# Linear attention into a maxout feed-forward on one core: the last-token conversions and the GpSimd-type products leave VectorE, and the order table is replaced

## The chip, the cores and the metric

One core of a Trainium2 chip runs the whole program in one launch. The time is device microseconds of that core. TensorE (PE) multiplies; VectorE (DVE), ScalarE (ACT) and GpSimd (POOL) do the work between the products; SyncE (SP) only issues DMAs. Lower is better. A change below about 0.3% (0.9 us here) cannot be told from no change.

## The reference

```python
def phi(x):                                   # q and k: 8 x 8 heads, 576 tokens, 64 wide
    proj = x @ w_phi                          # 64 -> 128
    proj = proj - max(abs(proj), axis=-1)
    return concat([exp(proj), exp(-proj)])    # 256 features
kv  = phi(k)^T @ v;   z = sum(phi(k))
att = (phi(q) @ kv) / (phi(q) @ z + 1e-6)     # 4608 tokens x 512 once the heads are joined
h   = max(att @ w1, att @ w2, att @ w3)       # 512 -> 768
out = h @ w_out                               # 768 -> 512
```

Inputs and output are float32; the products run in bfloat16.

## The kernel before, in words

**Attention** is cut into 16 units of four heads (`u` = 0 to 15, two units for each of the 8 batches). A unit's 576 tokens per head are 512 main tokens and 64 *last tokens*. Its q and k come by DMAs that convert to bfloat16 on the way (`Lq`, L373, and `Lk`, L378, both issued by GpSimd), its v by a plain float32 load (`Lv`, L413, issued by SyncE). The last tokens of q come apart, in float32 (`Lt`, L405), and one conversion, `C` (L408, tile `tail_raw` to `qk_bf`), puts them beside the k blocks. Units 0 to 3 are then turned on TensorE (L435, tile `tps`), with the copies back at L446 and L448; later units are turned by DMAs. Then follow the products with `w_phi` (L474, tiles `psk`, `pst`, `psq`; L574, `psm`), the largest magnitudes on VectorE (L478, tiles `mk`, `mq`), the exponentials on ScalarE (L482, L565), v times the factors of its rows (`va`, L529, tile `vab`, 1.1 us for half a unit and 2.1 us for a whole one on GpSimd), the product K (L548, `kvps`), its copies (L555, `kv_sb`), the product N (L605, `psn`), two VectorE steps and a reciprocal (L616, L619, L621) and the division `x` (L623, `x_sb`).

**Feed-forward** is nine chunks of 512 tokens. It uses max(a, b, c) = a + max(0, b - a, c - a): w1 is subtracted from w2 and w3 once, in six *differences of weights* (`wd`, L741, tile `w_bf`), each 256 columns wide, and w1 times w_out is made once (L752 to L766). The chunks then need two products each with the differences (`ups`, L662, 128x512, twelve groups of four), w1's part (L694) and the down product (L699). All of w1, w2, w3 and w_out come by four loads that GpSimd issues (`W`, L725): the tiles print as `w_bf` and `wout_bf`, and w2's load comes last.

**What sets the order.** A table of words, `PLAN` (L85 to L197), names for each of 1562 nodes its engine, its buffers and a start; on each engine instructions stand in the order of these starts. The starts themselves do nothing on the chip: across engines only data and buffers make anything wait. Where TensorE has a gap in the first part of the table, `fill` puts idle products (L804, tile `idler`). The line of a node that can run on several engines lists them with a cost (`costs`), and the table chooses one. The *ramp* is the time up to about 50 us, in which units 0 to 3 run, the weights arrive and the differences are made; from then on feed-forward chunks and attention units overlap.

Before, VectorE ran the last-token conversions of units 1, 2 and 3, three differences of weights and one division of unit 2.

Of the kernel before, what the change touches and what calls it, by code (L numbers as in the profile page):

```python
# [90 lines left out]
111T6@12.1 112D1@13.2 71A@13.0 1166G@13.1 109T1@13.3 113T0@13.8 76A@13.5 75A@14.0 154T76@14.0 50D@13.8 108S2@9.1 110D@14.4 114D@15.0 337S0@9.7
1165G@13.8 59A@14.5 137T43@14.7 139D1@15.2 115T10@15.3 157A1@14.7 82A0@15.1 57G@14.9 73A@15.2 118D1@15.8 62G@16.0 134T23@15.9 158A1@15.7 192D@16.4
56G@16.5 70A@16.2 136D@16.5 117A1@16.7 129T65@16.9 120A@17.2 133D@17.2 155A@17.6 138D@17.5 119A1@18.1 63T35@17.7 131A@18.6 65A0@18.8 135D@18.1
194T4@18.5 116A@19.0 122T25@19.2 61G@17.6 156A@19.5 189G@18.7 121D@18.7 132D@19.3 140A1@20.0 128D@19.6 60G@19.4 130A@20.2 195D2@20.2 64D@20.8
125D@21.0 142G1@20.5 159T01@19.7 126A@20.4 66T76@20.6 127A@20.9 163A@21.4 67D@21.6 267T4@21.3 144A@21.8 83T35@21.8 68D@21.8 88T76@22.2 141G@21.6
162A@22.0 268D3@22.0 161A@22.5 198T1@22.7 336G0@22.7 84D0@22.6 160A@23.0 265D@23.1 123A@23.5 89D1@23.2 164T4@22.8 85D@23.7 1177T3@23.3 143G@23.4
124A@24.0 166A0@24.4 148T07@23.9 199D@24.2 146G@23.6 1173T5@24.5 147G@24.6 165A@24.7 79T1@25.0 90D@24.4 150D1@24.9 1175T2@25.1 338G@24.8 1178A0@25.0
86D0@25.1 1174D@25.2 145G@25.0 167A1@25.9 149D@25.7 262G@26.1 80A1@26.0 1164G@26.8 273T64@25.6 168T75@26.1 81A@26.2 280T30@26.6 275A0@26.5 1176D@25.9
151T21@26.8 169D2@26.7 87G0@27.6 276D0@27.1 277A0@27.0 278A@27.4 152A@27.9 1179T7@27.5 282A@28.1 153D@27.7 91D1@27.9 170D@28.0 274A@28.5 92G@28.4
173T12@28.7 340S1@33.1 279D@28.5 171D2@29.1 172G1@29.4 174D0@29.3 1180A@29.0 98T5@29.1 1170G@30.3 99D@29.8 284A@29.5 178T64@29.3 179D1@30.1 193S3@34.6  # L100
175D@30.5 180D@31.0 1185T7@29.8 242T1@31.1 281A@30.0 100T5@31.2 93T62@31.4 196T4@31.9 406S1@35.2 176D0@31.5 285A@30.5 243A0@31.4 177G@32.4 286D@31.6
101A@31.7 94D2@32.2 95D@32.8 183T5@32.3 1186A@32.0 96D1@33.5 1181T0@32.5 97G@33.8 197A@32.5 244A@33.4 185T7@33.8 184A@33.7 283D@33.6 186D@34.2
181D2@34.5 1182A@34.1 207T62@34.1 182G@34.7 1172G@35.5 214T41@34.3 219T53@34.4 405G1@37.6 210D1@34.6 212A1@34.5 335G@38.3 1183T7@34.7 542G2@39.0 211A1@35.0
220D0@35.2 187T0@36.0 221D@35.8 209A@35.5 208A@36.0 404G@39.8 269T5@36.2 271T3@36.6 1184A@36.5 102T6@36.8 213D@36.4 272A@37.0 266S0@36.8 188D@37.0
103D@37.2 218D@37.5 215A@37.2 270A@37.5 200T27@37.1 217D@37.8 287T03@37.4 204A@38.4 1201T6@37.6 202A@38.9 1211T1@38.5 216A@39.4 290D@38.1 1169D@38.6
201A@39.6 288A@40.1 1167D@39.2 291D1@39.9 1199T5@39.4 1189T4@40.3 1200A1@40.5 206D@40.2 1168G@40.5 203D@40.8 1212D@41.4 289A@40.9 298A0@41.2 205A@41.4
474G3@42.6 341S@46.9 475S3@48.1 1190A@41.9 301A0@42.3 1191T3@41.1 1192D@42.2 222T50@42.1 223D@42.8 237T27@42.3 225A1@42.5 227G1@43.3 292T14@42.5 613S2@49.7
293D@43.4 240A1@42.7 241A1@43.2 239A@43.7 1193T3@42.9 1195T5@43.8 410S0@51.3 228G@45.4 1197T7@44.6 1194A@44.2 339S1@52.6 294D@44.0 238A@44.6 1196A@45.1
1198A@45.7 224D@44.6 310T14@45.6 1171D@45.5 313A0@46.2 295T32@45.8 226G@46.1 314A0@46.7 232T05@46.0 297D@46.2 233A@47.1 234A@47.6 407G@48.2 311A@48.1
1209T7@46.4 296D@46.8 312A@48.6 1202D@47.4 1210D@48.0 1205T2@47.2 349T43@48.2 473G@48.4 1206D@48.6 299G@49.2 355D0@49.2 229T60@48.4 235A@49.0 231D1@49.8  # L110
230D@50.2 352D@50.5 305T71@49.6 1203T2@49.9 318A1@49.5 236A@49.6 306A@50.1 1204D@51.1 1207T5@50.8 307A@50.6 300G@51.2 309A@51.1 409S@53.2 308A@51.5
1208D@51.8 256T06@51.6 246T72@52.1 315T1@52.5 245A0@52.0 353A1@52.1 257D0@52.4 247D2@52.9 476G@53.3 258D@53.4 350A@52.6 317A1@53.1 248D@53.8 1221T5@52.6
251T07@53.5 316A@53.3 351A1@53.6 478S2@54.6 354A@54.1 259D0@54.3 342T16@54.0 343A@54.6 252D1@54.4 253D@55.1 347A@55.0 344A@55.5 249D1@55.5 1222T@54.3
356T42@55.7 348D@55.6 358A@56.0 254D2@56.2 359D@56.4 1223A0@56.3 302T30@55.8 357A@56.8 1188G@53.5 614G0@55.0 260G2@55.2 250D@56.7 303A0@57.1 345D@57.2
1225T7@57.0 255G@57.2 360D1@57.7 479S@56.1 304A@57.4 324T54@57.9 325D0@58.5 346A@57.7 367A1@58.1 384T3@58.3 385A0@58.6 329T01@58.4 330D2@59.1 369G1@58.5
326D@59.6 379T26@59.0 386A@58.8 370A@59.1 319T53@59.3 1226T@59.7 543G@60.6 261S@58.0 411T04@61.1 381A1@59.4 320D1@60.0 327D0@60.5 380A1@59.9 383A@60.4
1224S@59.4 382A@60.8 331D@60.6 321D@61.1 374T25@61.3 332D1@61.5 328G1@61.3 544S0@60.0 364T16@61.5 1213T3@61.8 322D2@61.7 413A0@61.5 333G@62.0 323G@62.8
1227D1@61.8 368G@63.6 377A@62.0 1228S@62.6 376A@62.4 417D1@62.4 375A@62.9 365D@63.0 366D@63.6 1214T@62.7 1215D2@64.2 418T72@64.1 378A@63.4 425T15@64.3
429D0@64.8 1217T6@64.5 428D@65.2 1218T@65.4 415A0@63.9 334S@63.7 412A@64.4 611G@65.6 420A@64.8 421D@65.5 408S2@65.1 361T35@66.8 423A@65.3 414D@66.1
820S1@65.7 422A@65.8 419A@66.3 682S3@67.2 426A@66.7 427A@67.0 424D@66.7 416A@67.3 363D@67.3 1219A3@67.8 371T07@67.0 373A1@68.3 362D@67.9 372A@68.6  # L120
430T21@68.1 443T45@68.4 387A0@68.9 431D@68.6 445A0@69.0 487T63@68.6 489A1@69.4 444A0@69.9 545G@66.4 488A1@70.4 492A@70.9 436A0@71.3 1216S@68.8 437G0@71.7
398T70@69.0 1229T2@69.5 438G@73.8 548S3@69.4 432D@69.2 399D0@69.8 1230A0@71.5 393T17@70.4 394D2@71.0 395D@71.6 491A@72.0 1027S2@70.7 1235T4@70.8 447A@72.5
# [130 lines left out]
def kernel(  # L253
# [100 lines left out]
    def attention(u):  # L354
        un = units[u]
        b, ct0, h0 = u // 2, (u % 2) * 2, (u % 2) * HU
        by_pe = u < BY_PE

        def nd(kind, *args, **kw):
            return node(kind, u, *args, **kw)  # L360
# [157 lines left out]
        for t0, t1, of, need in ranges:  # L518
# [317 lines left out]
```

## Time and profile before

| | us |
|---|---|
| median of 3 runs (284.87 to 285.72) | 285.57 |
| the profiled execution | 285.78 |
| its span, first instruction to last | 284.0 |
| PE busy | 269.0 (95%) |
| VectorE busy | 221.7 (78%) |
| ScalarE busy | 197.4 (70%) |
| GpSimd busy | 150.3 (53%) |

1.8 us of the profiled time lie outside its span. GpSimd's issuing of a DMA counts as busy; SyncE's does not. Rows of a timeline give the start, the length of one merged run of equal instructions, the engine and line, and what it writes and reads.

### The profile page before, as it was taken

Reading aid. Unit: us, or ns where it says so; the run is one execution under the profiler, and the core shown is the slowest. Engines: PE = TensorE matmul, PEld = TensorE weight load, DVE = VectorE, ACT = ScalarE, POOL = GpSimd, SP = SyncE. Lnnn points to the kernel's source line nnn. Section 1 sums busy time; section 2 is a strip of 40 time slices with the busy share of each in tenths; the row PEclk is TensorE's granted clock in tenths of the full one; section 3 lists DMA queues with packets and bytes.
Section 4 is the critical chain, followed back from the end, with each engine's and each line's share of the span. In section 5 each row is a group of like instructions: output and inputs, shape, how many; then the busy total and the mean of one; then the engine's idle time right before and its main releaser. Section 6 shows DMA issues by size and latency. Waiting matters only on the chain.

```text
span 284.0 us, 8364 instructions
## 1 busy us (share of the span) xinstructions
PE 269.0 (95%) x3392; PEld 153.4 (54%) x3434; DVE 221.7 (78%) x439; ACT 197.4 (70%) x468; POOL 150.3 (53%) x164
## 2 busy tenths in 40 slices
PE   7958998999999999999999999999999999999993
PEld 5636764566646466555546655446556544444441
DVE  4998899999989899986899989998986942356210
ACT  3979598999999999799988888695789001020021
POOL 6488489986577868368575294171793500000000
PEclk9986799999999999999999999999999999999998
DMA  8999997999999999999969999640173241400153
GB/s 157 264 208 208 199 253 88 174 215 150 220 187 221 190 220 219 177 247 260 188 160 163 269 232 193 71 112 5 57 136 84 74 82 38 150 37 0 37 113 149
DMA packets 74679, 44.07 MB, mean 155 GB/s; under 512 B 51152, under 2 KB 65808, under 8 KB 74640
## 3 DMA queue, kind: packets, MB, share of 16 engines
q1 hardware_dynamic: 59568, 31.70, 52.3%
q0 software_dynamic: 14912, 11.77, 28.7%
q8 instruction: 27, 0.44, 0.7%
q14 instruction: 12, 0.10, 0.1%
q10 hardware_dynamic: 160, 0.07, 0.1%
HBM read 34.64 MB, written 9.44 MB: 155 GB/s over the span
## 4 chain that ended last, share of the span: by engine, by line
PE 76%; DVE 10%; DMA 5%; ACT 3%; issue 3%; POOL 1%; SPq 0%; POOLq 0%; DVEq 0%; ACTq 0%
PE ups L662 29%; PE ops L699 14%; PE ops L694 11%; PE kvps L548 6%; PE psn L605 5%; DMA v_raw<-in_v_dram 3%; PE psk L474 3%; DVE mk L478 3%; PE psm L574 2%; PE psq L474 2%; DVE mq L478 2%; DVE qk_bf L408 2%; DMA xT<-x_sb 1%; ACT Eq L565 1%; DMA k_raw<-in_k_dram 1%
## 5 line engine op out<-in xcount | busy, mean ns | idle before, releaser
L662 PE MATMUL ups<-xT,w_bf 128*128 128x512 bf16 x410 | 99.7, 379 | 2.4 <-DVE w_bf L741 0.9
L529 POOL TENSOR_TENSOR vab<-v_raw,em 128x1152 bf16<-128x1152 f32 (+1 forms) x36 | 68.8, 1922 | 28.4 <-ACT em L521 20.4
L482 ACT ACTIVATE Ek<-psk 128x512 bf16<-128x512 f32 x128 | 72.9, 644 | 5.9 <-PE psk L474 4.8
L565 ACT ACTIVATE Eq<-psm 128x512 bf16<-128x512 f32 x128 | 71.1, 627 | 4.1 <-PE psm L574 4.0
L662 PEld LDWEIGHTS <-w_bf 128*128 128x128 bf16 x432 | 39.9, 98 | 47.1 <-issue 2.0
L623 POOL TENSOR_TENSOR x_sb<-y,rden 128x384 bf16<-128x384 f32 x47 | 38.1, 825 | 31.7 <-DVE rden L621 31.4
L699 PE MATMUL ops<-wout_bf,hT 128*128 128x512 bf16 (+2 forms) x213 | 50.3, 373 | 0.9 <-issue 0.6
L671 DVE TENSOR_TENSOR hT<-hT,ups 128x512 bf16<-128x512 bf16 x54 | 35.9, 679 | 12.3 <-PE ups L662 8.9
L478 DVE TENSOR_REDUCE mq<-psq 128x4 f32<-128x512 f32 x64 | 41.7, 683 | 4.3 <-PE psq L474 4.2
L478 DVE TENSOR_REDUCE mk<-psk 128x4 f32<-128x512 f32 x64 | 42.5, 679 | 2.9 <-PE psk L474 1.5
L707 ACT COPY osb<-ops 128x512 f32<-128x512 f32 (+2 forms) x25 | 15.1, 607 | 34.7 <-PE ops L699 18.2
L675 ACT ACTIVATE hT<-ups 128x512 bf16<-128x512 f32 x32 | 19.3, 622 | 23.5 <-PE ups L662 17.3
L699 PEld LDWEIGHTS <-hT 128*128 128x128 bf16 x222 | 20.6, 98 | 22.9
L616 DVE TENSOR_TENSOR y<-psn,sq 128x390 f32<-128x390 f32 x48 | 26.3, 556 | 6.2 <-PE psn L605 4.2
L619 DVE TENSOR_TENSOR y<-y,psn 128x390 f32<-128x390 f32 x48 | 25.9, 554 | 2.1
L474 PEld LDWEIGHTS <-qkT 64*128 64x128 bf16 x576 | 18.7, 95 | 16.2 <-issue 12.3
L605 PEld LDWEIGHTS <-Eq 128*128 128x128 bf16 x512 | 21.4, 99 | 7.3 <-issue 0.4
L694 PE MATMUL ops<-xT 128*128 128x512 bf16 x88 | 24.0, 380 | 0.4
L548 PE MATMUL kvps<-vab,Ek 64*128 64x65 bf16 x1152 | 22.8, 195 | 1.7 <-DVE y L616 1.5
L548 PEld LDWEIGHTS <-Ek 64*128 64x128 bf16 x1152 | 21.1, 97 | 5.8 <-PE idler L804 2.8
L605 PE MATMUL psn<-kv_sb,Eq 128*128 128x65 bf16 x512 | 23.4, 195 | 0.1
L677 DVE TENSOR_SCALAR hT<-ups 128x512 bf16<-128x512 f32 x22 | 14.9, 683 | 7.7 <-PE ups L662 7.3
(73 smaller groups left out, 287.2 us busy)
## 6 DMA issues: line engine op xcount, KB each, us to landing
v_raw<-in_v_dram SPq DMA_DIRECT2D x16, 576.0 KB, 6.3
out_dram<-osb SPq DMA_DIRECT2D x32, 256.0 KB, 2.7
qk_bf<-in_k_dram POOLq DMA_DIRECT2D x15, 288.0 KB, 7.3
qk_bf<-in_q_dram POOLq DMA_DIRECT2D x15, 256.0 KB, 6.6
w_bf<-in_moe_w_dram POOLq DMA_DIRECT2D x3, 768.0 KB, 10.4
tail_raw<-in_q_dram SPq DMA_DIRECT2D x32, 32.0 KB, 5.5
wout_bf<-in_moe_w_out_dram POOLq DMA_DIRECT2D x1, 768.0 KB, 13.5
out_dram<-osb SPq DMA_DIRECT2D x6, 128.0 KB, 2.4
```

The lines of the kernel that those rows point to most:

```text
L474: nc.tensor.matmul(ps[s]()[:, i, :], lhsT=qkT()[r, n, :], rhs=wph[r, :], start=True, stop=True)
L478: return nd(kind, {"DVE": 0.598 if n == 4 else 0.331}, lambda: nc.vector.tensor_reduce(dst(m()), ps()[:, 0:n, :].rearrange("p (a j) f -> p ...
L482: return nd("ek", {"ACT": 0.478 if n == 4 else 0.264}, lambda: nc.scalar.activation(dst(Ek[g]()), ps()[:, 0:n, :], EXP, scale=1.0 - 2.0 * ...
L529: made.append(chosen(n_, lambda n_, g=g, t0=t0, t1=t1: (nc.vector if n_.eng == "DVE" else nc.gpsimd).tensor_tensor(vab()[:, g, t0:t1, 0:D] ...
L548: nc.tensor.matmul(kvps[ab]()[:, pr, g, :], lhsT=Ek[g]()[r, t, :], rhs=vab()[r, g, t, :], start=(pr == prs[0] and g + j == 0), stop=(pr == ...
L565: return nd("eq", {"ACT": 0.478 if n == 4 else 0.264}, lambda: nc.scalar.activation(Eq[g]()[:, t0:t0 + n, :], ps()[:, 0:n, :], EXP, scale= ...
L605: nc.tensor.matmul(o, lhsT=Eq[g]()[:, 8 * (c % 2) + 4 * pr + 2 * ab + c // 2, :], rhs=kv()[:, pr, ab, g, :], start=True, stop=True)
L623: divs.append(chosen(n_, lambda n_, th=th, y=y, rden=rden: (nc.vector if n_.eng == "DVE" else nc.gpsimd).tensor_tensor(x_sb()[:, 6 * th:6 ...
L662: nc.tensor.matmul(ups(), lhsT=w_bf[i + (not plain)][:, ct, j * P:(j + 1) * P], rhs=tokens_of(ct), start=(ct == 0), stop=(ct == CT - 1))
L671: nc.vector.tensor_tensor(dst, dst, src, ALU.max)
L694: nc.tensor.matmul(ops_()[:, 0:hi - lo], lhsT=tile_of(ct, tt), rhs=line_w(c_i > MOVE, ct, lo, hi), start=(ct == 0), stop=False)
L699: nc.tensor.matmul(ops_()[:, 0:hi - lo], lhsT=hT()[:, j, tt * P:(tt + 1) * P], rhs=wout_bf[:, j, lo:hi], start=plain and j == 0, stop=(j = ...
```

## The change

Three lines take VectorE from the engines on which some nodes may run: the last-token conversions `C` (GpSimd or ScalarE remain), v times its factors `va` and the division `x` (GpSimd alone). The table `PLAN` is new throughout, with 60 nodes on another engine. Everything that is computed stays.

```diff
 PLAN = """
-11S0@0.8 1D@0.8 14S@1.3 4A@1.1 13D0@4.0 12D@4.2 0G@1.2 3G@1.7 17S0@1.9 106S1@3.5 5A@1.8 8D@4.5 10G@2.2 20T0@4.6
...
+4A@1.1 11S0@0.8 3G@1.2 1D@0.8 14S@1.3 17S0@1.9 5A@1.8 0G@1.6 7A@4.1 9G0@2.2 12A@4.4 2G@2.9 13D@4.0 10G@3.1
...
@@ -404,7 +404,7 @@
         n_t = chosen(nd("Lt", {"SP": 1.24}, None, [], [t_raw], xfer=[(8, 18.0, 0.62)] * 2), load_t)
-        n_ = nd("C", {"POOL": 0.24, "DVE": 0.13, "ACT": 0.17} if by_pe else {"POOL": 0.24}, None, [n_t], [t_raw, qk_b], port=True)
+        n_ = nd("C", {"POOL": 0.24, "ACT": 0.17} if by_pe else {"POOL": 0.24}, None, [n_t], [t_raw, qk_b], port=True)
@@ -525,6 +525,7 @@
                 if u < BY_PE:
                     costs["DVE"] = 0.064 + 0.0667 * (t1 - t0)
+                costs = {"POOL": costs["POOL"]}
                 n_ = nd("va", costs, None, [n_em, main_v], [vraw, em, vab], port=True)
@@ -619,7 +620,7 @@
-            n_ = nd("x", {"POOL": 0.767, "DVE": 0.464} if by_pe else {"POOL": 0.767}, None, [n_], [y, rden, x_sb], port=True)
+            n_ = nd("x", {"POOL": 0.767}, None, [n_], [y, rden, x_sb], port=True)
```

After the change all lines behind L416 are one higher.

**VectorE, the stretch with unit 2's last tokens.** `mk` and `mq` are the largest magnitudes, `qkT` a copy of turned blocks, `qk_bf<-tail_raw` the last-token conversion. Before:

```order
L478 TENSOR_REDUCE mq<-psq 128x2x2
L478 TENSOR_REDUCE mk<-psk 128x4
L408 CAST qk_bf<-tail_raw 128x2x64
L478 TENSOR_REDUCE mq<-psq 128x2x2
L478 TENSOR_REDUCE mq<-pst 128x2
```

Now, around the same reductions:

```order
L446 COPY qkT<-tps 128x2x128
L478 TENSOR_REDUCE mk<-psk 128x4
L478 TENSOR_REDUCE mq<-psq 128x2x2
L478 TENSOR_REDUCE mk<-psk 128x4
L478 TENSOR_REDUCE mk<-pst 128x2
L448 COPY qkT<-tps 128x1024
```

No conversion of last tokens is left on VectorE: those of units 0, 1, 2 and 3 stand on GpSimd.

**VectorE, the differences of weights** (`w_bf<-w_bf`). Before:

```order
L637 COPY xT<-pxT 128x384 x2
L478 TENSOR_REDUCE mq<-pst 128x2
L478 TENSOR_REDUCE mk<-pst 128x2 x2
L741 TENSOR_TENSOR w_bf<-w_bf 128x4x256 x2
L478 TENSOR_REDUCE mq<-pst 128x2
L478 TENSOR_REDUCE mk<-psk 128x4 x2
L671 TENSOR_TENSOR hT<-hT,ups 128x512
```

Now:

```order
L638 COPY xT<-pxT 128x384
L742 TENSOR_TENSOR w_bf<-w_bf 128x4x256
L478 TENSOR_REDUCE mk<-psk 128x4 x2
L742 TENSOR_TENSOR w_bf<-w_bf 128x4x256 x2
L478 TENSOR_REDUCE mq<-psq 128x2x2 x2
L678 TENSOR_SCALAR hT<-ups 128x512
L742 TENSOR_TENSOR w_bf<-w_bf 128x4x256
L672 TENSOR_TENSOR hT<-hT,ups 128x512
```

VectorE makes four differences in place of three: one of w3, then two of w2, then one of w3.

**GpSimd, the same place.** `x_sb` is the division, `qk_bf<-in_...` are issues of loads. Before:

```order
L623 TENSOR_TENSOR x_sb<-y,rden 128x384 x3
L741 TENSOR_TENSOR w_bf<-w_bf 128x4x256
L378 DMA qk_bf<-in_k_dram 128x2x576
L373 DMA qk_bf<-in_q_dram 128x4x256 x3
L741 TENSOR_TENSOR w_bf<-w_bf 128x4x256
L378 DMA qk_bf<-in_k_dram 128x2x576
L529 TENSOR_TENSOR vab<-v_raw,em 128x18x64
```

Now:

```order
L726 DMA w_bf<-in_moe_w_dram 128x4x768
L624 TENSOR_TENSOR x_sb<-y,rden 128x384 x2
L378 DMA qk_bf<-in_k_dram 128x2x576
L624 TENSOR_TENSOR x_sb<-y,rden 128x384
L742 TENSOR_TENSOR w_bf<-w_bf 128x4x256
L624 TENSOR_TENSOR x_sb<-y,rden 128x384
L373 DMA qk_bf<-in_q_dram 128x4x256
L742 TENSOR_TENSOR w_bf<-w_bf 128x4x256
L378 DMA qk_bf<-in_k_dram 128x2x576
L530 TENSOR_TENSOR vab<-v_raw,em 128x18x64 x2
```

Of the row of four issues one stands ahead of GpSimd's last difference (of w2, which waits for w2's load and nothing else), one behind it, and two moved behind the products of v.

More of the change, by code (lines that the diff above doesn't have):

```diff
@@ L91 @@
[L91 to L98, printed above, removed]
@@ new lines @@
+23D@7.9 34A@7.8 8D@8.3 104G@8.5 29D@8.5 37T56@8.4 24T7@8.7 107G@9.3 36D@8.7 32A@8.3 25D@9.3 44T03@9.1 337S2@5.1 19S1@6.7
+79T4@9.3 47D@9.6 38A@8.8 26T1@9.4 190G2@9.6 39A@9.3 42A@9.8 40D@9.9 55A0@10.3 43D@10.5 1163G@10.3 263G3@11.0 69T27@9.7 189G@11.8
+58G0@12.5 81A0@10.5 27D@11.1 72A0@10.7 109T5@10.7 110D1@11.5 191S3@7.3 1166G@12.6 73A0@11.2 48D0@12.1 52T17@11.9 192G@13.4 80A@11.7 41A@12.0
+53D@12.4 70A@12.4 57G@13.6 71A@12.9 264S0@8.8 59A@13.4 115T45@12.2 121D1@13.0 46A@13.6 49T36@12.6 51D@13.6 108S2@10.4 50D@14.2 62G@14.7
```

210 lines of the change are left out of this document (107 added, 103 removed).

## The prediction

> **What bounds the kernel now.** I read the page first, then the stretches by window, then VectorE's and GpSimd's rows in time, then the chain of waits.
>
> ```profile
> span 284.0 us, 8364 instructions
> PEclk9986799999999999999999999999999999999998
> DMA  8999997999999999999969999640173241400153
> ```
>
> The span is 284.0 us and TensorE's clock dips only in slices 3 to 5. The DMA engines are nearly full for the first half. The windows (us, then PE, PEld, DVE, ACT, POOL busy, PE clock, DMA share, GB/s) tell the ramp from the rest:
>
> ```profile
> 3.75:17.00 13.25, 11.63 (x136) 7.68 (x134) 12.46 (x28) 10.72 (x28) 7.43 (x11) 1.00 1.16 226
> 17.00:19.00 2.00, 0.33 (x4) 0.19 (x3) 2.00 (x2) 2.00 (x6) 1.99 (x4) 0.98 1.16 209
> 19.00:25.60 6.60, 6.09 (x107) 4.54 (x107) 5.38 (x13) 4.30 (x14) 4.14 (x5) 0.50 1.21 208
> 25.60:27.20 1.60, 1.51 (x33) 1.27 (x30) 1.60 (x3) 1.60 (x4) 1.60 (x5) 0.96 1.19 220
> 27.20:29.00 1.80, 0.31 (x8) 0.16 (x8) 1.80 (x3) 1.80 (x5) 1.80 (x3) 1.00 1.24 193
> 29.00:32.70 3.70, 3.70 (x67) 3.16 (x67) 2.95 (x8) 0.78 (x4) 1.64 (x3) 0.54 1.30 191
> 32.70:45.00 12.30, 12.14 (x193) 8.33 (x193) 11.66 (x31) 11.80 (x26) 9.22 (x9) 1.00 0.91 194
> 50.00:100.00 50.00, 49.26 (x753) 28.32 (x758) 46.68 (x94) 48.80 (x119) 39.09 (x40) 1.00 1.21 196
> 100.00:150.00 50.00, 49.10 (x787) 28.61 (x795) 43.78 (x90) 45.26 (x109) 33.81 (x34) 1.00 1.09 208
> 150.00:200.00 50.00, 49.31 (x679) 28.10 (x682) 45.43 (x92) 39.03 (x93) 22.33 (x24) 1.00 0.80 145
> 200.00:279.00 79.00, 78.37 (x629) 39.47 (x637) 42.96 (x79) 25.41 (x59) 19.13 (x21) 1.00 0.30 79
> ```
>
> From 50 us on TensorE is idle for 0.74, 0.90, 0.69 and 0.63 us: 2.96 us in 229. There it is the bound, and a us won before that place reaches the end, if the order behind it is as good. The ramp is another case: twice TensorE runs dry (0.33 us busy of 2.00, 0.31 of 1.80) while VectorE shows 100%, and each time the clock halves for some us after. VectorE's rows say why:
>
> ```profile
> 9.72 0.22 DVE L408 CAST qk_bf<-tail_raw 128x128 bf16<-128x128 f32 x1
> 16.46 2.48 DVE L408 CAST qk_bf<-tail_raw 128x128 bf16<-128x128 f32 x1
> 26.57 1.84 DVE L408 CAST qk_bf<-tail_raw 128x128 bf16<-128x128 f32 x1
> 44.93 2.65 DVE L741 TENSOR_TENSOR w_bf<-w_bf 128x1024 bf16<-128x1024 bf16 x2
> 52.84 0.68 DVE L741 TENSOR_TENSOR w_bf<-w_bf 128x1024 bf16<-128x1024 bf16 x1
> ```
>
> The same conversion takes 0.22 us when GpSimd is idle and 2.48 and 1.84 us when it is not; two differences of weights take 2.65 us where two of 0.68 us would take 1.36. What GpSimd did then:
>
> ```profile
> 15.90 2.29 POOL L529 TENSOR_TENSOR vab<-v_raw,em 128x576 bf16<-128x576 f32 x2
> 18.11 0.81 POOL L373 DMA_DIRECT2D qk_bf<-in_q_dram  x1
> 18.93 1.17 POOL L529 TENSOR_TENSOR vab<-v_raw,em 128x576 bf16<-128x576 f32 x1
> 26.92 0.28 POOL L408 CAST qk_bf<-tail_raw 128x128 bf16<-128x128 f32 x1
> 27.18 1.14 POOL L529 TENSOR_TENSOR vab<-v_raw,em 128x576 bf16<-128x576 f32 x1
> 29.08 0.75 POOL L725 DMA_DIRECT2D w_bf<-in_moe_w_dram  x1
> 36.57 2.13 POOL L741 TENSOR_TENSOR w_bf<-w_bf 128x1024 bf16<-128x1024 bf16 x1
> 43.97 0.77 POOL L378 DMA_DIRECT2D qk_bf<-in_k_dram  x1
> 44.73 2.25 POOL L373 DMA_DIRECT2D qk_bf<-in_q_dram  x3
> 46.97 2.59 POOL L741 TENSOR_TENSOR w_bf<-w_bf 128x1024 bf16<-128x1024 bf16 x1
> 52.88 2.62 POOL L529 TENSOR_TENSOR vab<-v_raw,em 128x1152 bf16<-128x1152 f32 x1
> ```
>
> VectorE's conversion begun at 16.46 ends at 18.94, with GpSimd's two products and its issue behind it; the pair at 44.93 stands beside three issues that end at 46.98. The blocking goes both ways: GpSimd's difference at 46.97, begun while VectorE's second one ran, takes 2.59 us against 2.13. So the two engines exclude each other for these forms, and whoever comes second waits, sometimes for several instructions.
>
> **The change part by part.** *The stalls.* The three conversions leave VectorE: 2.48 - 0.22 = 2.26 us and 1.84 - 0.22 = 1.62 us of stall go, the first one costs nothing now. The differences' stall is 2.65 - 1.36 = 1.29 us. Together 5.17 us of VectorE's ramp, and the halved clock behind two of them, which I don't price apart: what counts is when the ramp ends. On GpSimd a conversion costs 0.28 us (the row at 26.92), four of them 1.1 us; their cover is GpSimd's own idle time in the ramp, 13.25 - 7.43 us up to 17 us alone. Without that cover the 1.1 us would delay the products of v and so product K.
>
> *The mark.* I take the first product that needs a difference of w2, the tile loaded last. The chain of waits around it:
>
> ```profile
> 45.02 1.98 DVE w_bf L741
> 46.99 0.05 issue
> 47.04 2.76 PE ups L662 x12
> ...
> 266.52 0.86 PE ups L662 x4
> ```
>
> It starts at 47.04. When can it start now? w2's load sets a floor. It was issued at 29.08 and landed after
>
> ```profile
> DMA to landing us min/median/max: 9.2/9.2/9.2
> ```
>
> that is at 38.3, while VectorE came to the difference 6.6 us later. GpSimd issues the same twelve loads ahead of it as before, in another order, and the DMA share was 1.16 to 1.30 without a pause up to then, so I keep 38.3 (bounds: 37.5, if SyncE's loads move behind it, and 39.5, if the queue once runs empty for the length of an issue or two).
>
> *VectorE's floor.* From 3.75 to 45 us it is busy 12.46 + 2.00 + 5.38 + 1.60 + 1.80 + 2.95 + 11.66 = 37.85 us, 33.97 without the two stalls. By the order, what moves off it ahead of the mark (conversions, four copies of `kv_sb`, one large copy of turned blocks, three reductions) and what moves on (two large copies, two of `xT`, two reductions, a difference) come to about the same. So it reaches the difference between 3.75 + 33.97 = 37.7 us, never idle, and 41.1 us, with the 3.4 us of idle that it had.
>
> *GpSimd's floor.* GpSimd's own difference of w2 waits for that load alone, and nothing in GpSimd's queue holds it: it starts at about 38.4 and, by the 2.13 us of its kind, ends at 40.5. Nothing keeps the two engines in the table's order. VectorE's difference finds GpSimd at work unless it comes first. Between the ends (38.4 if VectorE is first, 41.3 if the issue of 0.77 us behind GpSimd's difference goes ahead of it too) I take 40.5: two reductions stand ahead of it on VectorE, and GpSimd stands waiting when the load lands. Then 0.68 us of difference: the product starts at 40.5 + 0.68 = 41.2, against 47.04. That is 5.8 us.
>
> *What is missing then.* Ahead of the mark TensorE had done two products with w3's differences, now one: 0.86 us (the last row) more to do. It has done two wide products `psm` and one group of `psq` more and three smaller groups less, about 0.2 us the other way. Left: 5.8 - 0.86 + 0.2 = 5.2 us. Behind the mark VectorE has two differences in both orders, and GpSimd one (2.1 us) less.
>
> *Behind the ramp.* The division that moves from VectorE to GpSimd lies where GpSimd is busy 39.09 us of 50, and is hidden there; without cover it costs its 0.8 us. The order after the ramp is new too, and some loads do not come earlier because the ramp does. I have no row for that. The bounds are the idle time of TensorE behind the ramp once less and once more, -3.0 to +3.0; I take +0.9, the idle of the one worst stretch (100 to 150) again.
>
> *Sum.* 5.2 - 0.9 = 4.3 us: 285.78 - 4.3 = 281.5 for the profiled execution; the median lay 0.2 us below that, so **281.3 us**.
>
> *A page against this change.* At 44.93 the trace has 1.29 us of stall of two differences beside three issues of loads. The Trainium skill ("SBUF — State Buffer", section on the two separate sides) has it that a VectorE instruction with two SBUF inputs is shut out only by a GpSimd instruction that reads SBUF, which an issue does not do. By it keeping the differences clear of issues would win nothing, and the sum would be smaller by at most that 1.29 us (282.6); the trace shows the stall, so I go by the row. On GpSimd's own difference, which reads SBUF, page and row agree.
>
> **The rivals.**
>
> *VectorE comes first* at w2's difference, or the load lands when GpSimd is still at an issue. Then the product starts at 38.4 + 0.68 = 39.1: 7.9 - 0.66 - 0.9 = 6.3 us, 279.3 us. For it: 37.7 is possible for VectorE. Against: 3.4 us of idle would have to go too. 0.17.
>
> *The ramp gets a new thin place.* GpSimd takes its casts in order and each waits for its tail load; the new order has 34 products of units 0 and 1 in a row without an idle product among them, and dry stretches of 1.8 and 2.0 us halved the clock for 3.7 and 6.6 us. If one such spell comes back with its stall, 2 us of the 4.3 go: 283.3 us. Against: no conversion stands on VectorE any more. 0.13. The Trainium skill ("TensorE: Matmul & The Clock Gate", Part 1) puts the idle time that halves the clock at about 3.4 us; by that this rival would need a longer gap, but here 1.8 us, not quite idle, did it.
>
> *A difference falls behind v's products: slower.* VectorE's fourth difference now comes close to where GpSimd starts two whole products of v, a cast and two issues without a break: 2.1 + 2.1 + 0.3 + 0.8 + 0.8 = 6.1 us. If GpSimd is first and VectorE gets no turn in between, as at 16.46 and 26.57, VectorE and all reliefs of `ups` stand for 6.1 us: 281.3 + 6.1 = 287.4 us. It decides as soon as ScalarE has made unit 2's factors, which start the product, before VectorE reaches that difference. Against: ScalarE's factors stand behind a relief of a product that itself waits for w2's difference, so both are late together; and at 52.84 VectorE came first by 0.04 us and GpSimd took the wait (2.62 us). 0.11.
>
> *It doesn't do what it says*: the stalls only move, to other pairs of the same forms, since nothing but timing keeps them apart: 285.6. Against: of VectorE's thirteen instructions of these forms (six conversions of k and of the weights of phi, three of last tokens, three differences, one division) seven are left. 0.06.
>
> **How the numbers follow.** The forecast has 0.53. Its own range is 280 to 282.7: a load at 37.5 or 39.5, an issue of 0.77 ahead, half of the bounds behind the ramp. The range 279.0 to 285.3 takes in the first two rivals and leaves out the slower one and some of the rest. Faster by over 0.3% (below 284.7): 0.53 + 0.17 + 0.11 of the thin place = 0.81; slower (above 286.4): 0.11 + 0.01; the same: 0.07. 0.3% is what a measurement of this kernel can tell.
>
> **What would show it.** No `qk_bf<-tail_raw` on VectorE; TensorE's clock at 1.00 from 17 to 33 us, with no window of 2 us under 0.35 busy; w2's load landing at about 38; GpSimd's difference of w2 ahead of VectorE's, which then lasts about 2 us; the first `ups` behind it at 41 us; TensorE idle about 3 to 4 us from 50 us on. Wrong it would be if that product started after 45 us, or if it started at 41 and the end did not follow: then the order behind the ramp has eaten it.

## The result and the profile after

The changed kernel took 280.44, 284.18, 281.96 and 280.45 us: a median of 281.2 us (4 runs) against 285.42 us (4 runs, 284.87 to 285.72) of the kernel before. The ratio is 0.9863 [0.9817, 0.9908], so it is 0.9% to 1.8% faster. The prediction was 281.3 us, with 0.81 on faster.

Medians below leave disturbed executions out, and of one profiled execution that was disturbed (of e9, below) only rows ahead of 55 us are read.

The profiled execution is the one of 280.44 us. Two lines of its page, beside those shown of before:

```profile
span 278.6 us, 8375 instructions
PEclk9999999999999999999999999999999999999999
```

The dip of TensorE's clock in slices 3 to 5 is gone, and the span is 5.4 us shorter. The windows of the changed kernel (us, then PE, PEld, DVE, ACT, POOL busy, PE clock, DMA share, GB/s):

```profile
17.00:19.00 2.00, 1.83 (x52) 1.20 (x50) 1.85 (x5) 1.78 (x8) 2.00 (x3) 1.00 1.15 206
19.00:25.60 6.60, 6.28 (x142) 4.95 (x143) 6.60 (x15) 6.60 (x18) 6.57 (x9) 1.00 1.28 205
27.20:29.00 1.80, 1.74 (x41) 1.54 (x34) 1.67 (x5) 1.77 (x6) 1.46 (x2) 1.00 1.21 210
29.00:32.70 3.70, 3.65 (x57) 2.55 (x56) 3.70 (x12) 3.70 (x9) 1.69 (x3) 1.00 1.17 209
50.00:100.00 50.00, 48.99 (x805) 28.79 (x807) 45.99 (x96) 45.50 (x111) 39.02 (x43) 1.00 1.15 201
100.00:150.00 50.00, 49.44 (x727) 28.49 (x735) 45.59 (x93) 43.82 (x106) 33.43 (x32) 1.00 1.09 195
150.00:200.00 50.00, 49.31 (x679) 28.02 (x687) 43.91 (x89) 39.74 (x94) 26.60 (x29) 1.00 0.64 132
```

Where TensorE was busy 0.33 us of 2.00 and 0.31 of 1.80, it is now busy 1.83 and 1.74, and both spells at half the clock (0.50 for 6.6 us, 0.54 for 3.7 us) are at 1.00. From 50 to 200 us it is idle for 1.01 + 0.56 + 0.69 = 2.26 us, against 0.74 + 0.90 + 0.69 = 2.33 before: nothing that this shows was lost behind the ramp. Both sums are too high, though. The profiles of before and of the changed kernel hold 3392 and 3391 matrix products to 3434 and 3433 weight loads, so 42 products lack a record, and their time shows as idle; in the changed kernel's other profile (e1), which holds 3433 of both, the same three windows are idle for 0.18 + 0.03 + 0.00 = 0.21 us. The place of the differences, by the rows in time of VectorE, GpSimd and TensorE:

```profile
37.55 0.68 DVE L742 TENSOR_TENSOR w_bf<-w_bf 128x1024 bf16<-128x1024 bf16 x1
39.34 2.12 DVE L742 TENSOR_TENSOR w_bf<-w_bf 128x1024 bf16<-128x1024 bf16 x2
43.47 0.68 DVE L742 TENSOR_TENSOR w_bf<-w_bf 128x1024 bf16<-128x1024 bf16 x1
37.01 0.81 POOL L373 DMA_DIRECT2D qk_bf<-in_q_dram  x1
38.20 2.11 POOL L742 TENSOR_TENSOR w_bf<-w_bf 128x1024 bf16<-128x1024 bf16 x1 [0.38 <-DMA w_bf<-in_moe_w_dram]
45.27 2.11 POOL L530 TENSOR_TENSOR vab<-v_raw,em 128x1152 bf16<-128x1152 f32 x1 [4.26 <-ACT em L521]
40.92 2.76 PE L663 MATMUL ups<-xT,w_bf 128*128 128x512 bf16 x12 [0.55 <-DVE w_bf L742]
```

w2's load lands at 38.2; GpSimd, which waited for it, takes its difference first; VectorE's pair of w2 lasts 2.12 us instead of 1.28, and the product behind it starts at 40.92 us (47.04 before, 41.2 predicted).

### The profile page after: what moved, and what is told of

It reads as the page before. It is cut to its first block, busy times and chain, and to the rows that moved or that the text cites. A ratio compares the mean times of both kernels' runs of the same rounds, so it can differ in the third digit from the quotient of the medians.

```text
span 278.6 us, 8375 instructions
## 1 busy us (share of the span) xinstructions
PE 266.4 (96%) x3391; PEld 150.2 (54%) x3433; DVE 216.6 (78%) x435; ACT 196.3 (70%) x467; POOL 149.8 (54%) x169
## 4 chain that ended last, share of the span: by engine, by line
PE 81%; ACT 11%; DVE 3%; issue 2%; DMA 1%
PE ups L663 32%; PE ops L700 15%; PE ops L695 11%; PE kvps L549 6%; PE psn L606 5%; ACT Ek L482 5%; ACT Eq L566 4%; PE psm L575 3%; PE psk L474 3%; PE psq L474 2%; PE psn L611 1%; DMA wphi_f<-in_w_phi_dram 1%; DVE mk L478 1%; PE idler L805 1%; PE pst L474 1%
## 5 line engine op out<-in xcount | busy, mean ns | idle before, releaser
L566 ACT ACTIVATE Eq<-psm 128x512 bf16<-128x512 f32 x128 | 72.9, 627 | 8.5 <-PE psm L575 8.2
L624 POOL TENSOR_TENSOR x_sb<-y,rden 128x384 bf16<-128x384 f32 x48 | 39.2, 823 | 33.5 <-DVE rden L622 33.2
L676 ACT ACTIVATE hT<-ups 128x512 bf16<-128x512 f32 x34 | 20.1, 616 | 24.7 <-PE ups L663 17.7
L708 ACT COPY osb<-ops 128x512 f32<-128x512 f32 (+1 forms) x23 | 13.3, 583 | 32.2 <-PE ops L700 32.2
L474 PEld LDWEIGHTS <-qkT 64*128 64x128 bf16 x576 | 18.0, 94 | 16.4 <-issue 11.5
L678 DVE TENSOR_SCALAR hT<-ups 128x512 bf16<-128x512 f32 x20 | 13.7, 683 | 12.1 <-PE ups L663 11.9
L549 PE MATMUL kvps<-vab,Ek 64*128 64x65 bf16 x1152 | 21.8, 191 | 0.4 <-issue 0.4
L549 PEld LDWEIGHTS <-Ek 64*128 64x128 bf16 x1152 | 20.2, 94 | 2.2 <-issue 0.5
```

What stands on the lines that cost most here:

```text
L474: nc.tensor.matmul(ps[s]()[:, i, :], lhsT=qkT()[r, n, :], rhs=wph[r, :], start=True, stop=True)
L549: nc.tensor.matmul(kvps[ab]()[:, pr, g, :], lhsT=Ek[g]()[r, t, :], rhs=vab()[r, g, t, :], start=(pr == prs[0] and g + j == 0), stop=(pr == ...
L566: return nd("eq", {"ACT": 0.478 if n == 4 else 0.264}, lambda: nc.scalar.activation(Eq[g]()[:, t0:t0 + n, :], ps()[:, 0:n, :], EXP, scale= ...
L624: divs.append(chosen(n_, lambda n_, th=th, y=y, rden=rden: (nc.vector if n_.eng == "DVE" else nc.gpsimd).tensor_tensor(x_sb()[:, 6 * th:6 ...
```

## The experiments

They ran in three groups, each on one chip with its own runs of the kernel before: e1 to e4 (before 285.76 us), e5 to e9 (285.67), e10 to e13 (285.36). Chips differ by up to 0.4 us in the kernel before, so runs of different groups are compared by their ratios. e4 and e5 have one execution each. "idle 38:45" is TensorE's idle time in us in that window of the profiled execution.

| run | what it is | median us (runs) | ratio to before | profiled us | idle 38:45 |
|---|---|---|---|---|---|
| e1 | the changed kernel again | 283.36 (11) | 0.992 [0.9885, 0.9954] | 282.71 | 2.04 |
| e2 | before + three conversions to GpSimd | 280.65 (4) | 0.9868 [0.98, 0.9937] | 279.68 | 0.92 |
| e3 | changed + GpSimd's w2 difference to VectorE | 280.26 (4) | 0.9834 [0.9783, 0.9884] | 280.45 | 0.00 |
| e4 | e3 + four issues beside the differences | one execution | | 281.21 | 0.08 |
| e5 | changed + four issues ahead of GpSimd's difference | one execution | | 283.39 | 1.30 |
| e6 | e3 + unit 2's conversion back | 283.08 (10) | 0.9912 [0.9872, 0.9951] | 282.71 | 0.08 |
| e8 | e2 + GpSimd's w2 difference to VectorE | 280.95 (4) | 0.984 [0.9793, 0.9887] | 280.35 | 0.06 |
| e9 | before + that difference alone | 285.97 (8) | 1.0001 [0.9973, 1.0028] | | 0.00 |
| e10 | before + unit 2's conversion alone | 284.27 (9) | 0.9972 [0.9941, 1.0003] | 285.41 | 0.01 |
| e11 | before + unit 3's conversion alone | 282.5 (5) | 0.9915 [0.988, 0.9951] | 283.04 | 0.92 |
| e12 | e3 without idle products behind 12 us | 281.43 (10) | 0.9883 [0.985, 0.9916] | 281.86 | 0.08 |
| e13 | e8 + w3's last difference taken forward | 281.83 (3) | 0.9881 [0.9821, 0.9941] | 281.83 | 0.19 |

### e1: the changed kernel again

No edit.

> The changed kernel once more, unchanged, for the spread of its time. Four executions gave 280.44, 280.45, 281.96 and 284.18 us, the last with a mean TensorE clock of 0.985 over its span against 0.998 in the profiled one. Theory (the gain is the ramp's stalls, and one spell of halved clock still comes up now and then): most executions at 280.4 to 282, few at 283 to 285 and those with a clock below 0.99. Rival (the times scatter for another reason): the clock does not tell the slower executions from the others.

Only one execution of the twelve lies below 282.4 us, so the expectation was a miss, and the gain of 1.4% is here 0.8%. The profiled one has its clock at 1.00 in every window of the table above; what stands out are the differences, in VectorE's, GpSimd's and TensorE's rows in time:

```profile
38.33 2.99 DVE L742 TENSOR_TENSOR w_bf<-w_bf 128x1024 bf16<-128x1024 bf16 x1
42.44 1.28 DVE L742 TENSOR_TENSOR w_bf<-w_bf 128x1024 bf16<-128x1024 bf16 x2
37.80 0.81 POOL L373 DMA_DIRECT2D qk_bf<-in_q_dram  x1
38.63 2.13 POOL L742 TENSOR_TENSOR w_bf<-w_bf 128x1024 bf16<-128x1024 bf16 x1
41.38 1.04 PE L663 MATMUL ups<-xT,w_bf 128*128 128x512 bf16 x4 [1.20 <-DVE w_bf L742]
43.17 2.76 PE L663 MATMUL ups<-xT,w_bf 128*128 128x512 bf16 x12 [0.76 <-DVE w_bf L742]
```

VectorE's difference of *w3* began at 38.33, beside GpSimd's issue of a q load, and ended at 41.32 only, behind GpSimd's whole difference of w2. In the first profile the same pair stood so too (37.55 beside 37.01 to 37.82) and took 0.68 us. What differed is w2's load: there it landed at 38.2, behind VectorE's start; here it was issued at 28.6 and landed 8.9 us later, at 37.5, so GpSimd's difference stood ready behind the issue when VectorE began. The ramp was about 0.8 us later in this execution, and the load 0.7 us earlier. On these two profiles it is the order of landing and start that goes with 0.68 or 2.99 us; e4 and e5 below test the cause. The product of w2 started at 43.17, 2.25 us later than in the first profile.

That isn't all of the scatter. Time and mean granted clock of all sixteen executions of the changed kernel, from their records:

```
us     280.32 280.44 280.45 281.96 282.44 282.59 282.71 282.81
clock    .999   .998   .998  1.000   .997   .997   .997   .998
us     283.36 283.60 283.69 283.74 283.77 284.05 284.18 284.75
clock    .993   .993   .993   .994   .985   .985   .985   .994
```

All executions from 283.36 us on have a lower clock (the kernel before has mostly 0.978 to 0.988). So some us at a lower clock came back in half of them; where, is not recorded. And 282.44 to 282.81 us stand at the same clock as 280.44, so the clock alone does not make the scatter either.

### e2: the conversions alone

The table of before, with three words changed:

```diff
-107D1@9.7 ... 192D@16.4 ... 265D@23.1
+107G1@9.7 ... 192G@16.4 ... 265G@23.1
```

> The kernel before with its own table; only the last-token conversions of units 1, 2 and 3 go from VectorE to GpSimd, at the same starts. Theory (the two conversions' stalls of 2.26 and 1.62 us and the halved clock behind them make most of the loss): no dry stretch of TensorE at 17 to 19 and 27 to 29 us, clock 1.00 throughout, VectorE at its first difference of w2 at 38.5 to 41 us in place of 44.93, the stall beside GpSimd's issues or its difference of w2 (1.3 to 2.6 us) stays; time 280.5 to 282.5 us. Rival (the new table is what makes the gain, the conversions alone are worth little): 284 to 285.5 us.

280.65 us, as expected, and TensorE's clock is 1.00 in all windows from 17 to 32.7 us: the conversions by themselves bring all that the change brings, and the new table adds nothing that these runs show. Its differences still stall, in the rows in time of VectorE, GpSimd and TensorE:

```profile
39.16 2.65 DVE L741 TENSOR_TENSOR w_bf<-w_bf 128x1024 bf16<-128x1024 bf16 x2
38.96 2.25 POOL L373 DMA_DIRECT2D qk_bf<-in_q_dram  x3
41.20 2.59 POOL L741 TENSOR_TENSOR w_bf<-w_bf 128x1024 bf16<-128x1024 bf16 x1
41.27 2.76 PE L662 MATMUL ups<-xT,w_bf 128*128 128x512 bf16 x12 [0.92 <-DVE w_bf L741]
```

It is the picture of before, 5.8 us earlier: 2.65 us for two differences beside a row of issues.

### e3 and e4: differences without GpSimd's, and beside issues

```diff
 e3, on the changed table
-1167G@40.1
+1167D@40.05
 e4, on e3
-404G@48.3 ... 542G3@49.1 ... 473G@51.8 ... 543G@58.8
+404G@42.85 542G3@42.87 473G@42.89 543G@42.91
```

> The changed kernel, but GpSimd's one difference of w2 is made by VectorE too, behind its two others, so that no tensor instruction of GpSimd stands beside them. Theory (the two engines exclude each other; GpSimd's difference holds VectorE's first one, which began at 39.34 and let the product go at 40.92): VectorE's differences of w2 take 0.68 us each, the first product behind them starts at 40.1 us, 0.8 us earlier; VectorE has 0.68 us more to do; time from 0.8 us faster to the same as the changed kernel. Rival (the 1.5 us of that difference is a wait for data): the product stays at 40.9 us and the time gets 0.7 us longer.

> As the run with all differences of w2 on VectorE, but four more issues of loads by GpSimd (q of units 5, 6 and 7, k of unit 7) are moved ahead, so that GpSimd issues six loads in a row, about 37.0 to 41.6 us, beside VectorE's differences and with no tensor instruction near. Theory (issues shut VectorE's differences out, as the 1.29 us of stall at 44.93 in the kernel before say): the differences from 39.3 us on take together 1.3 us or more longer than three of 0.68 us, 3.3 us and above in place of 2.0. Rival (an issue does not read SBUF and shuts nothing out; the one at 37.55 in the changed kernel ran 0.68 us beside an issue): 2.0 to 2.2 us for the three.

VectorE's and TensorE's rows of e3:

```profile
39.80 1.88 DVE L742 TENSOR_TENSOR w_bf<-w_bf 128x1024 bf16<-128x1024 bf16 x3
39.78 3.63 PE L663 MATMUL ups<-xT,w_bf 128*128 128x512 bf16 x16
```

VectorE's and GpSimd's rows of e4:

```profile
40.07 1.88 DVE L742 TENSOR_TENSOR w_bf<-w_bf 128x1024 bf16<-128x1024 bf16 x3
39.23 2.27 POOL L373 DMA_DIRECT2D qk_bf<-in_q_dram  x3
41.47 0.73 POOL L378 DMA_DIRECT2D qk_bf<-in_k_dram  x1
```

In e3 three differences take 1.88 us together, and the four executions lie within 0.44 us (280.01 to 280.45), where the changed kernel's on the same chip spread over 3.7. The first four of the sixteen products in the row at 39.78 are w3's; in the trace the weights of w2's are loaded from 40.53 us on, behind a wait of 0.20 us for VectorE's first difference, and the product starts at 40.66, 0.26 us earlier than in the changed kernel's first profile and not the 0.8 expected. The time is 280.26 against 283.36 us of the changed kernel on the same chip, and the intervals of the ratios just part. From before's table with the three conversions moved (e2) it cannot be told. In e4 the same three differences stand beside four issues and again take 1.88 us. So issues alone shut nothing out here, as e4's rival had it. The prediction had read the row at 44.93 of before as issues that block; that reading fell.

### e5: a ready difference behind the issues

```diff
 on the changed table
-474G2@42.8 ... 404G@48.3 ... 542G3@49.1 ... 473G@51.8
+474G2@39.5 404G@39.6 542G3@39.7 473G@39.8
```

> The changed kernel, with four issues of loads (one of k, three of q) put ahead of GpSimd's difference of w2 instead of behind it, so that this difference, whose load lands at 38.1, stands ready behind a row of issues, as GpSimd's last difference did in the kernel before at 44.93. Theory A: VectorE's two-input difference is shut out while an issue runs with a ready SBUF instruction queued behind it. Then VectorE's first difference of w2, begun at 39.3, lasts to the end of the issues at about 41.2 (1.9 us), or to the end of GpSimd's difference behind them (43.3, 4 us), and the first `ups` product of w2 starts at 41.2 to 43.4. Rival B: issues shut nothing out, whatever is queued (as in the run where four issues stood beside differences of 0.68 us each): VectorE's first difference takes 0.68 us, the product starts at 40.0.

VectorE's, GpSimd's and TensorE's rows in time:

```profile
39.83 4.16 DVE L742 TENSOR_TENSOR w_bf<-w_bf 128x1024 bf16<-128x1024 bf16 x2
38.98 2.27 POOL L373 DMA_DIRECT2D qk_bf<-in_q_dram  x3
41.23 2.20 POOL L742 TENSOR_TENSOR w_bf<-w_bf 128x1024 bf16<-128x1024 bf16 x1
41.52 1.90 PE L663 MATMUL ups<-xT,w_bf 128*128 128x512 bf16 x8 [0.67 <-DVE w_bf L742]
44.05 1.04 PE L663 MATMUL ups<-xT,w_bf 128*128 128x512 bf16 x4 [0.63 <-DVE w_bf L742]
```

Against e4, the difference of w2 is back on GpSimd, behind the row of issues. VectorE's first difference now lasts until the issues end (the product that needs it starts at 41.52), its second until GpSimd's own is done (the next product starts at 44.05). So what shuts VectorE out is an issue *with a ready difference queued behind it*: more than data and buffers makes one engine wait for another here. Why GpSimd holds VectorE off ahead of that instruction's own recorded start, no trace shows. The one execution took 283.39 us.

### e6: one conversion back

```diff
 on e3
-192G@13.4
+192D@15.55
@@ the node of C
-{"POOL": 0.24, "ACT": 0.17}
+{"POOL": 0.24, "DVE": 0.13, "ACT": 0.17}
```

> The kernel with both differences of w2 on VectorE (280.26 us), with only the conversion of unit 2's last tokens put back on VectorE, at 15.5 us, beside four of GpSimd's products of v in a row (15.9 to 19.3 us). Theory A: it is shut out until the row ends, some 2 to 3.6 us in place of 0.22; TensorE runs dry for about 2 us behind it and the clock halves for some us, as in the kernel before: 2.3 us of stall and the halved clock together, 284 to 285.5 us. Rival B: the stall comes, but not the halved clock, since TensorE has other work by then: plus 2.3 us, 282.5 us. Rival C: the stall lies in VectorE's slack ahead of w2's load (landed 38.1, difference 39.8): 280.3 to 281 us.

VectorE's and GpSimd's rows in time:

```profile
15.72 1.85 DVE L408 CAST qk_bf<-tail_raw 128x128 bf16<-128x128 f32 x1
15.20 3.39 POOL L530 TENSOR_TENSOR vab<-v_raw,em 128x576 bf16<-128x576 f32 x3
```

Two of its windows, with the columns as above:

```profile
17.00:18.00 1.00, 0.00 (x0) 0.00 (x0) 1.00 (x2) 1.00 (x3) 1.00 (x2) 1.00 1.13 205
20.00:21.00 1.00, 1.00 (x30) 1.00 (x31) 1.00 (x3) 0.58 (x3) 1.00 (x2) 0.50 1.38 201
```

A stall of 1.85 - 0.22 = 1.63 us, one dry us of TensorE behind it, then half the clock: 283.08 us, 2.8 us more than e3 by the medians and 2.2 by the ratios. The clock is theory A's, the time nearer to rival B's 282.5. VectorE got its turn behind the second of GpSimd's three products, not behind the row. The two executions whose mean clock was 1.00 took 280.40 and 280.41 us, as e3 did; the other eight, at 0.978 to 0.997, took 281.94 to 284.27. Whether those two had the stall is not recorded, so e6 prices stall and clock together.

### e8, e9 and e13: the differences' stalls

```diff
 e8 on e2, and e9 on before
-1168G@40.5
+1168D@39.85
 e13 on e8
-1171D@45.5
+1171D@39.9
```

> The table of before with the three conversions on GpSimd (280.65 us) and, besides, GpSimd's difference of w2 moved to VectorE, behind VectorE's own. In the run of the conversions alone the first difference took 2.04 us beside issues with GpSimd's difference queued behind them. Theory A: without that difference in GpSimd's queue nothing is shut out: three differences of 0.68 us, the first product of w2 at 39.9 in place of 41.27, 279.3 to 280.0 us. Rival B: issues alone still shut it out: first difference 2 us, product at 41.3, 280.6 us. Rival C: the product starts at 39.9, but w3's products then wait, or the order behind takes it back: 280.3 to 280.7.

> The kernel before, its conversions where they were, with only GpSimd's difference of w2 moved to VectorE, behind VectorE's own; so the issues of loads stay beside VectorE's differences. Theory A: what shut VectorE's difference out at 44.93 was the ready difference queued behind the issues, so the stall goes: three differences of 0.68 us, the first product of w2 at 45.7 in place of 47.04, 284.1 us against 285.4 of before; the stalls of the conversions and the halved clock stay. Rival B: the issues themselves shut it out: the first difference keeps its 2 us, the product starts at 47.0, 285.4 us or 0.6 us more for the third difference.

> The table of before with the three conversions on GpSimd, GpSimd's difference of w2 on VectorE, and the last difference (of w3) taken forward, so that all four stand on VectorE within 1.2 us of reductions, before GpSimd's products of v begin (43.8 us in the last run of this kind, where that difference, at 46.05, took 2.60 us beside such a product). Theory A: all four take 0.68 us, the 1.9 us of stall at 46 go, and the time is 279.3 to 280.3 us. Rival B: the two reductions and the relief of `ups` that now come 0.6 us later cost as much, or TensorE was busy anyway: 280.3 to 281.0 us.

VectorE's differences in e8, with GpSimd's product of v beside the last one:

```profile
39.13 1.89 DVE L741 TENSOR_TENSOR w_bf<-w_bf 128x1024 bf16<-128x1024 bf16 x3
46.05 2.60 DVE L741 TENSOR_TENSOR w_bf<-w_bf 128x1024 bf16<-128x1024 bf16 x1
45.99 2.11 POOL L529 TENSOR_TENSOR vab<-v_raw,em 128x1152 bf16<-128x1152 f32 x1
```

VectorE's in e9, and GpSimd's issues beside the first three:

```profile
44.98 2.24 POOL L373 DMA_DIRECT2D qk_bf<-in_q_dram  x3
45.18 1.88 DVE L741 TENSOR_TENSOR w_bf<-w_bf 128x1024 bf16<-128x1024 bf16 x3
52.10 2.59 DVE L741 TENSOR_TENSOR w_bf<-w_bf 128x1024 bf16<-128x1024 bf16 x1
```

VectorE's in e13:

```profile
40.32 1.89 DVE L741 TENSOR_TENSOR w_bf<-w_bf 128x1024 bf16<-128x1024 bf16 x3
42.46 0.68 DVE L741 TENSOR_TENSOR w_bf<-w_bf 128x1024 bf16<-128x1024 bf16 x1
```

With no difference left on GpSimd at that place, three of VectorE's take 1.88 us beside the same issues, which is theory A for the stall. e9's row of twenty products with differences starts at 44.46 us, the first eight of them w3's, so w2's product starts at about 46.2 instead of 47.04. But the stall came back 7 us later, when w3's last difference met a product of v (2.60 us), and the times did not move: e9 285.97 us against 285.67 of before, e8 280.95 against 280.65 of e2 (ratios 0.984 and 0.9868, within each other's intervals). That alone leaves open whether the second stall took back what the first gave. e13 has no stalled difference at all and took 281.83 us, longer than both its expectations, and can't be told from e8 either (0.9881). Its profiled execution had half the clock from 17 to 19 us, with no conversion on VectorE; but its two others, at 0.999 and 1.000 of the clock, took 281.99 and 281.09, which is not below the medians of e2 and e8. So with before's table the differences' stalls are not what the end waits for. With the new table it is otherwise: there e3, without them, is 3.1 us below the changed kernel by the medians, though a part of that is the changed kernel's lower clock in some executions.

### e10 and e11: one conversion at a time

```diff
 e10 on before
-192D@16.4
+192G@16.4
 e11 on before
-265D@23.1
+265G@23.1
```

> The kernel before with one conversion alone moved to GpSimd: that of unit 2 (2.48 us at 16.46 on VectorE). All three moved gave 280.65 us against 285.85. Theory A: each stall has its own price, as the prediction's terms have it: 2.26 us and the halved clock behind it go, the spell at 27 to 32 us stays: 282.7 to 283.5 us. In the trace TensorE's clock is 1.00 from 19 to 25.6 and still near 0.5 behind 28. Rival B: the first spell is hidden by what is late anyway (the second stall, w2's load), and this conversion alone brings less than 1 us: 285 us.

> The kernel before with the conversion of unit 3 alone moved to GpSimd (1.84 us at 26.57 on VectorE). Theory A: 1.62 us of stall and the second spell of halved clock go, the first stays: 283 to 283.8 us; this gain and that of unit 2's alone add up to about the 5.2 us of the three together. Rival B: whichever is left sets the end, and one alone brings less than 1 us: 285 us.

The conversion that remains on VectorE in e10:

```profile
23.29 3.10 DVE L408 CAST qk_bf<-tail_raw 128x128 bf16<-128x128 f32 x1
```

e10's windows:

```profile
19.00:25.60 6.60, 4.64 (x92) 3.20 (x92) 6.60 (x11) 6.60 (x20) 6.27 (x10) 1.00 1.20 208
25.60:27.20 1.60, 0.29 (x12) 0.29 (x13) 1.60 (x3) 0.79 (x2) 1.60 (x3) 0.54 1.17 212
29.00:32.70 3.70, 3.70 (x74) 3.18 (x71) 2.74 (x5) 2.23 (x5) 0.38 (x1) 0.52 1.34 204
```

The one that remains in e11 took 2.41 us at 16.49, as before. e11's windows:

```profile
19.00:25.60 6.60, 5.94 (x104) 4.38 (x104) 5.42 (x12) 4.11 (x14) 3.95 (x4) 0.50 1.21 208
29.00:32.70 3.70, 3.60 (x86) 2.51 (x83) 3.61 (x9) 3.55 (x11) 2.88 (x4) 1.00 1.26 184
```

Each removes its own spell of half clock and leaves the other, as theory A has it. The times: unit 2's conversion alone brings 1.1 us by the medians (0.28% [0, 0.6%] by the ratio), between its two expectations, unit 3's alone 2.9 us (0.85% [0.5%, 1.2%]), more than either. With unit 2's away, unit 3's came 3.3 us earlier and met a longer row of GpSimd's work: 3.10 us in place of 1.84, so a part of the first gain was handed to the second stall. 1.1 + 2.9 = 4.0 us against 5.1 of the three together (285.76 - 280.65); the intervals don't tell this from a plain sum.

### e12: without the idle products

```diff
 on e3
-WARM = 30.0
+WARM = 12.0
```

> The kernel with both differences of w2 on VectorE (280.26 us), without the ten idle products that TensorE makes between 12 and 30 us by the table. No work of the reference is left out. It asks for the price of the halved clock without any stall. Theory A: where the conversions stall nobody, TensorE has no stretch of 2 us under 0.35 busy, the clock stays at 1.00 and the time at 280.3 us (up to 280.8). Rival B: the idle products carried it: a window between 12 and 25 us shows a clock near 0.5 for 3 to 6 us, and the time is 2 to 4 us longer, 282 to 284 us.

Two windows of e12:

```profile
17.00:19.00 2.00, 1.21 (x15) 0.95 (x16) 1.65 (x4) 2.00 (x7) 2.00 (x3) 0.50 1.15 206
19.00:25.60 6.60, 6.60 (x156) 5.90 (x151) 5.80 (x13) 5.79 (x18) 6.57 (x9) 0.68 1.28 204
```

They show the clock of rival B without a stalled conversion. The time is 281.43 us, between the two expectations: 1.2 us more than e3 by the medians and 1.4 by the ratios, though by the windows 2.00 x 0.50 + 6.60 x 0.32 = 3.1 us of full clock went. All ten executions have a mean clock of 0.982 to 0.988; five of them took 280.74 to 281.01 us, the others up to 283.76. By the medians half clock alone is cheaper than stall and clock together (e6: 2.8 us), but the intervals of e3, e12 and e6 overlap, so neither price is firm.

## Why the prediction was right, and where it was not

**The conversions' stalls and the clock: right, and they are the whole gain.** e2 has it with three words of the table, e6 loses 2.8 us by undoing one. The prediction's two terms of 2.26 and 1.62 us were lengths of stalls, not prices: alone they brought 1.1 and 2.9 us, since the stalls hand time to each other and each drags a spell of half clock behind it. "Which I don't price apart" left out a size: about 1.2 us for one spell by e12's median, with a wide scatter.

**The mark: each step right in the first profile.** Load at 38.3 (38.2 measured), GpSimd's difference of w2 first (38.20 to 40.31), VectorE's first of w2 behind it, 1.52 us long where about 2 was forecast, product at 41.2 (40.92), TensorE's clock at 1.00 from 17 to 33 us. In e1's profile the load landed at 37.5, at the prediction's lower bound, and the product started at 43.17 all the same: the sum had no term for w3's difference being held up.

**The sum: the term behind the ramp was mis-sized.** "-0.9" stood for idle time of TensorE behind 50 us, read from a profile in which 42 products lack a record. From the mark to the end it was 0.1 us: in the first profile the mark gave 47.04 - 40.92 - 0.86 + 0.2 = 5.5 us and the end 285.78 - 280.44 = 5.3, in e1's 3.2 and 3.1. The profiled execution therefore came out at 280.44 us where the sum had 281.5: 0.3 us of it is the earlier mark, the rest this term. That the median of four fell on 281.2 is partly luck: it is pulled up from 280.4 by slower executions, for reasons that the term did not mean. With e1's executions the median of fifteen is 282.8 us, 1.5 above the forecast and just outside the prediction's own range of 280 to 282.7, though inside 279.0 to 285.3.

**"VectorE's stall of 1.29 us at the differences": wrong in cause and in worth.** Issues don't shut VectorE out (e4); a ready difference queued behind them does (e5, and e2 against e8). And with before's table, where it was priced, removing that stall moved no time (e8, e9, e13). In the changed kernel 2.12 - 1.28 = 0.84 us of it remained anyway.

**The mark as the currency of the end: only half right.** Between the changed kernel's two profiles it holds: 2.25 us in the mark, 2.27 in the end. Between kernels it doesn't. e3 starts its product of w2 0.26 us earlier than the changed kernel's first profile and ends together with it (280.45 and 280.44 us); e2 starts it 0.35 us later and ends 0.8 us earlier; e5 starts it 0.6 us later and ends 2.95 us later, as its second difference holds the next product back to 44.05; and e9's comes about 0.85 us earlier than before's for no gain that its interval shows. The table's last column sorts these profiles better: up to 0.9 us of idle time of TensorE between 38 and 45 us (0.59 in the changed kernel's first profile), the times lie from 279.7 to 281.2, and with 1.3 and 2.0 us (e5, e1) they are 283.4 and 282.7. (e6 and e9 to e13 had half the clock earlier.) It gives an order and no price, since e5 lost less here than e1 and ended later. That a late difference is hidden as long as TensorE has other products to make is argued from this and not shown. What sets the common floor at about 280.3 us is not settled.

**The rivals.** *VectorE first* was priced as a gain of 2 us. In e1 VectorE did begin first, with w3's difference and by 0.3 us, and lost: "whoever comes second waits" does not hold by the recorded starts. *The thin place* (283.3 us, 0.13): half of sixteen executions have the lower clock and 283.4 us or more, so its chance was put too low; since the time at the differences scatters as well (e1), its price is not separated. *The slower one* did not happen here, since v's product started at 45.27, 1.1 us behind the end of w3's last difference; where it did (e8, e9) the difference took 2.60 us and the time did not move, against the 6.1 us that were priced. *It doesn't do what it says* holds for the differences alone.

**The page against the change.** The prediction weighed the Trainium skill ("SBUF — State Buffer", section on the two separate sides) against the row at 44.93 and went by the row. For an issue alone the page is right (e4: 1.88 us for three), and by it keeping the differences clear of issues wins nothing; e8 and e9, where three take 1.88 us beside the issues, agree. It would not have told of the stall in e5, though: the same section lets whichever instruction starts first keep the port, and in e1 the difference begun at 38.33 waited for one begun at 38.63.

## What to carry to other kernels

When VectorE's copy or two-input instruction is longer than its kind, look on GpSimd not only at the instruction beside it but at the next one in its queue, and whether that one's data are there; here a load that landed 0.8 us ahead of VectorE's start or 0.7 us behind it went with 2.99 or 0.68 us. Price a stall by what TensorE does meanwhile: the ones that left it dry cost 1.1 and 2.9 us with the half clock behind them (e10, e11), one at the differences cost nothing with before's table (e9, e13). And where a change has parts, the part with three words may hold all of the gain, so try it alone before a new table.

## What was not expected of the hardware

- A row of DMA issues on GpSimd left VectorE's two-input differences at 0.63 us each (e4), but with a ready SBUF difference queued behind the issues the first took until the issues ended (e5, before, e2), or, in e1, until that difference itself had ended (2.99 us). Which of the two it is, these runs don't explain.
- TensorE's clock was halved behind thin stretches, not only dry ones. These windows of e12 lead to it:

```profile
14.00:15.00 1.00, 0.48 (x9) 0.30 (x9) 1.00 (x3) 1.00 (x5) 1.00 (x3) 1.00 1.18 229
15.00:16.00 1.00, 0.67 (x6) 0.10 (x2) 1.00 (x3) 1.00 (x4) 1.00 (x3) 1.00 1.20 221
16.00:17.00 1.00, 0.36 (x4) 0.17 (x4) 1.00 (x3) 1.00 (x4) 1.00 (x2) 0.70 1.18 210
```

  No us is dry, and the clock is at half from about 16.4 us on. The Trainium skill ("TensorE: Matmul & The Clock Gate", Part 1) speaks of an idle window of about 3.4 us; here three us at 0.36 to 0.67 busy, 1.51 us in all, went ahead of it. The sum alone does not decide: in the same three us e13 was busy for 1.86 us (0.65, 0.76, 0.45) and halved its clock from about 16.6 on, and e8, with 1.85 (0.55, 0.49, 0.81), kept it at 1.00.
